# A recurrent attention and two routed mixtures: a chunk's output rows move ahead of the next chunk's values, and the places of the first mixture wait three turns longer

## The chip, the cores and the metric

The kernel runs on one core of one Trainium2 chip. The metric is the device time of one launch in microseconds. Three runs of the kernel before gave 523.09, 523.45 and 524.38 us; the median is 523.45 us.

## The reference

Three parts follow each other. The first is a linear attention with a decaying state, for 4 batches, 8 heads, 768 positions and 48 values per head:

```python
for t in range(S):
    state = alpha[:, :, t, :, None] * state + np.einsum('bhd,bhe->bhde', k[:, :, t], v[:, :, t])
    y[:, :, t] = np.einsum('bhd,bhde->bhe', q[:, :, t], state)
```

Its output, seen as 3072 rows of 384 values, goes through a mixture of 8 experts (384 to 1024 to 384, a relu between). Only rows with a positive skip score are computed; each is sent to the expert with the greatest logit and weighted by that expert's probability. The result is added to the row:

```python
logits = xc @ w_gate
e_idx = np.argmax(logits, axis=1)
h = np.maximum(xc[mask] @ w1[e], 0.0)
y[mask] = gate_w[mask, None] * (h @ w2[e])
out[do_compute] = xc + y
```

A second mixture of the same size, without the skip and without the addition, makes the output.

## The kernel before

**Attention.** The positions are cut into 24 chunks of 128 (0 to 23 here), six per batch. The first chunk of a batch has no state to add, and the last one makes none. For chunk g three helpers issue the work. `emit_a(g)` multiplies keys and queries into two PSUM banks, `ap0` and `ap1` (line 566); VectorE masks the first (`at`, line 574), ScalarE copies the second and GpSimd masks it (line 572). Then TensorE transposes the keys (`kp`, line 581) and ScalarE copies them (`ks`). `emit_y(g)` makes the chunk's outputs (`yp`, lines 605 to 615) and the next state (`sp`, lines 599, 610, 611); ScalarE takes both out (`y`, line 618, and `s`, line 623). `emit_r(g)` turns the outputs into rows of 384 values and 17 logits with four matmuls (`rp`, line 645). ScalarE copies the rows to `xy` (line 646), a DMA stores them, and VectorE sums the logits into `lg` (line 648). `prep(g)` runs two scans over alpha on VectorE (lines 546 and 550), and GpSimd multiplies keys and queries with them (lines 554 and 555).

**Order.** Each engine works its instructions off in the order in which the program issues them. One turn of the attention loop (line 747 on) issues `emit_a(g + 1)`, `prep(g + 3)`, `emit_y(g)`, `emit_r(g - 1)`. In the attention the tiles `ap0`, `ap1`, `sp`, `yp` and `rp` share four PSUM banks that are handed out in turn, so a tile waits for the last reader of an earlier one.

**Routing.** Small instructions on VectorE find each row's expert and its place among the expert's rows. They are generators in a list. `rt(n)` moves waiting ones on by a step or more; `release(w)` counts a tick (a turn) up and moves on those that asked for TensorE's turn (`yield 1`) more than w ticks ago; `finish` runs named ones to their end. In the attention a group of rows is routed after chunks 5, 11, 17, 20 and 23. `index` (line 340) ends each: VectorE makes a table `hot` (line 372), and some ticks later TensorE multiplies it into `idx_ps` (line 377). The argument `nl` is 16 for the groups of the attention and 8 for those of the first mixture (`gate_rows`).

**Mixtures.** Nine stages (j from 0 to 8) each put one block of gathered rows through one expert: `ffn1` (lines 463 to 469, `hh` and `hl` are the two halves of the hidden layer), then `ffn2t` (lines 487 to 489). Each tile of weights comes by a DMA into `raw`, and ScalarE with VectorE or GpSimd splits it into two halves (lines 202 and 207). The rows of stage j are routed for the second mixture during the stages behind it. The second mixture has nine stages as well; its first three blocks of rows are gathered (line 441) by what the last routings found.

Of the kernel before, what the change touches and what calls it, by code (L numbers as in the profile page):

```python
# [59 lines left out]
RT1B = (3, 3, 3, 3, 3, 3, 3, 3, 3, 3, 3, 3)  # L60
REL1B = (4, 4, 4, 6, 6, 6, 6, 6, 6, 6, 6, 4)
RELS = (7, 2, 2)
STEPS = (1, 1, 1)
STEPS2 = (3, 2, 3)
FIN2 = (0, 3)
# [43 lines left out]
def body(tc, qka, vN, rw, wg2, wg17, w1a, w2a, w1b, w2b, cst, zr, out):  # L109
# [3 lines left out]
    with ctx:  # L113
# [6 lines left out]
        def cc(name):  # L120
            o, w = CST[name]
            return cs[:, o:o + w]
# [12 lines left out]
        with ExitStack() as fctx, tc.manual_schedule():  # L135
# [25 lines left out]
            def spot(name, w, *shape, bufs=2):  # L161

                if name not in spots:
                    spots[name] = [used[0], 0]
                    used[0] += w * bufs
                    assert used[0] <= 512
                p = spots[name]
                n = int(np.prod(shape))
                assert n <= w
                o = p[0] + w * (p[1] % bufs)  # L170
                p[1] += 1
                v = own[:, o:o + n]
                if len(shape) == 2:
                    v = v.rearrange("p (a b) -> p a b", a=shape[0])
                elif len(shape) == 3:
                    v = v.rearrange("p (a b c) -> p a b c", a=shape[0], b=shape[1])
                return v
# [38 lines left out]
            def background(n=1):  # L216
                for _ in range(n):
                    if bg:
                        split_w(*bg.pop(0))

            active = []
            turn = [0]

            def step(r):
                tok = next(r[0], None)
                if tok is None:
                    active.remove(r)  # L230
                else:
                    r[1] = turn[0] if tok == 1 else None
                return tok != 2

            def rt(n=1):
# [14 lines left out]
            def start(gen):  # L250
                r = [gen, None]
                active.append(r)
                return r

            def finish(*which):

                while any(r in active for r in which):
                    release()
                    rt()
# [61 lines left out]
            def wait(what, i):  # L321

                while done[what] < i:
                    yield 2
# [14 lines left out]
            def index(i, n, nl, ohm, on, rk, cols, region, first, last):  # L339

                ad = sm.tile([128, n, nl], F32, tag=f"ad{nl}", name="ad")
                V.tensor_tensor(ad, rk, ohm, op=ALU.mult)
                held[0] = False
                yield 0
                r = sm.tile([128, n, 1], F32, tag=f"r{nl}", name="r")
                V.tensor_reduce(r[:, :, 0], ad, axis=AX.X, op=ALU.add)
                yield 0
                ge = sm.tile([128, n, 4], F32, tag=f"ge{nl}", name="ge")
                V.tensor_tensor(ge, r.to_broadcast([128, n, 4]), kept["th"].rearrange("p (o e) -> p o e", o=1).to_broadcast([128, n, 4]), op=ALU.is_ge)
                yield 0  # L350

                tl = spot("tl", 6, n, 1)
                V.tensor_reduce(tl[:, :, 0], ge, axis=AX.X, op=ALU.add)
                yield 0
                ti = spot("ti", 48, n, 2, 4)
                V.tensor_tensor(ti, cc("seq")[:, 0:4].rearrange("p (a o e) -> p a o e", a=1, o=1).to_broadcast([128, n, 2, 4]),
                                tl.rearrange("p a (o e) -> p a o e", o=1).to_broadcast([128, n, 2, 4]), op=ALU.is_equal)
                yield 0
                pm = spot("pm", 6, n, 1)
                V.scalar_tensor_tensor(out=pm, in0=tl, scalar=-128.0, in1=r, op0=ALU.mult, op1=ALU.add)  # L360
                w = 8 * sum(t for _, t in cols)
                mv = sm.tile([128, n, 2, w], F16, tag=f"mv{nl}", name="mv")
                o = 0
                for j0, t in cols:
                    V.tensor_tensor(
                        mv.rearrange("p a h c -> p (a h) c")[:, :, o:o + 8 * t].rearrange("p a (e t) -> p a e t", t=t),
                        on.rearrange("p a h e -> p (a h) e")[:, :, j0:j0 + 8].rearrange("p a (e o) -> p a e o", o=1).to_broadcast([128, 2 * n, 8, t]),
                        ti.rearrange("p a h t -> p (a h) t")[:, :, 0:t].rearrange("p a (o t) -> p a o t", o=1).to_broadcast([128, 2 * n, 8, t]), op=ALU.mult)
                    o += 8 * t
                yield 0  # L370
                hot = sm.tile([128, n, 128], F16, tag=f"hot{nl}", name="hot")
                V.tensor_tensor(hot, cc("iota").rearrange("p (o c) -> p o c", o=1).to_broadcast([128, n, 128]), pm.to_broadcast([128, n, 128]), op=ALU.is_equal)
                yield 1
                yield from wait("indexed", i)
                done["indexed"] += 1
                for k in range(n):
                    T.matmul(idx_ps[:, region, :, NCOL - w:], lhsT=hot[:, k, :], rhs=mv[:, k], start=(first and k == 0), stop=(last and k == n - 1))
                if last:
                    yield 0
                    yield 0  # L380
# [152 lines left out]
            def load_v(g):  # L533
                if g >= NB:
                    return
                vt[g] = wk.tile([128, NP, 2 * D], F32, tag="v", name="v", bufs=4)
                SY.dma_start(vt[g], vN[g])
# [181 lines left out]
            def halves_of(w, hi, lo):  # L719
                A.activation(out=hi, in_=w, func=AF.Copy, scale=SX)  # L720
                V.scalar_tensor_tensor(out=lo, in0=w, scalar=SX, in1=hi, op0=ALU.mult, op1=ALU.subtract)
# [26 lines left out]
            for g in range(NB):  # L748
                if g + 1 < NB:
                    emit_a(g + 1)  # L750
                if g + 3 < NB:
                    prep(g + 3, whole)
                emit_y(g)
                if g > 0:
                    emit_r(g - 1)
                    i, k, n, _ = gof[g - 1]
                    if k == n - 1:
                        finish(*routes[max(i - 2, 0):max(i - 1, 0)])
                        routes.append(start(route(i)))
                if g == 0:  # L760
                    A.activation(out=upper, in_=cc("upper"), func=AF.Copy)
                    A.activation(out=ones, in_=cc("ones"), func=AF.Copy)
                    for name, w in (("desc", 8), ("tok", NB), ("seq", 8)):
                        kept[name] = spot(name, w, w, bufs=1)
                        V.tensor_copy(kept[name], cc(name))
                    nb = NB + len(TILES1)
                    kept["th"] = spot("th", 4, 4, bufs=1)
                    V.tensor_copy(kept["th"], cc("th")[:, 1:5])
                    kept["num"] = spot("num", 2 * nb, nb, 2, bufs=1)
                    V.tensor_scalar(kept["num"][:, :, 0], cc("pcol").to_broadcast([128, nb]), 1.0, None, op0=ALU.add)  # L770
                    V.tensor_copy(kept["num"][:, :, 1], cc("blk"))
                    kept["one"] = spot("one", 1, 1, bufs=1)
                    V.memset(kept["one"], 1.0)
                if g == 3:
                    halves_of(wg2s, rg[:, :, 128:136], rg[:, :, 136:144])
                    for k in range(3):
                        P.tensor_copy(rg[:, k, 0:128], ident)
                load_v(g + 3)
                load_qka(g + 5)
                if g >= NB - 2:  # L780
                    turn1(0, g - NB + 2)
                if g == NB - 1:
                    emit_r(g)
                    finish(*routes[:-1])
                    routes.append(start(route(len(GROUPS) - 1)))
                rt(RT[g])
                if g in (3, 6):
                    load_w(0, g // 6)
                if g >= 6 and g % 2 == 0:
                    background()  # L790
# [125 lines left out]
            def tick(f):  # L916
                release(REL1[f] if j == 0 else RELS[min(j, 2)])
                background(f % 2 if j > 1 else 0)
                rt(RT1[f] if j == 0 else STEPS[min(j, 2)])

# [312 lines left out]
```

## Time and profile before

| | |
|---|---|
| median of three runs | 523.45 us |
| the profiled execution, whole | 524.4 us |
| its span, first to last instruction | 522.7 us |
| TensorE busy (matmuls) | 490.9 us, 94% |
| VectorE busy | 353.7 us, 68% |
| ScalarE busy | 270.3 us, 52% |
| GpSimd busy | 267.2 us, 51% |

Busy times are sums over the whole span. The attention fills the first 149 us, the first mixture reaches to about 287 us, the second fills the rest. The profile's names are PE for TensorE's matmuls, DVE for VectorE, ACT for ScalarE and POOL for GpSimd; L574 is line 574 of the kernel before. An entry in square brackets is how long the engine stood idle ahead of the instruction, and what ended that.

### The profile page before, as it was taken

To read this page: it belongs to the slowest core of one execution; us is meant where nothing else is said; L and a number is where in the kernel's file an instruction comes from. 1 tells how busy PE (TensorE), PEld (TensorE's weight loads), DVE (VectorE), ACT (ScalarE), POOL (GpSimd) and SP (SyncE) were. 2 spreads that over 40 slices of the span, in tenths; PEclk is the share of its full clock that TensorE was granted. 3 is DMA by queue.
4 is the path that set the end of the run, shared out by engine and by line. 5 is a ranking of instruction groups with operands and counts; after the bars stand their busy time and mean duration, and the time that the engine had idled before them with its cause. 6 is when DMAs were issued, how large, how long until landed. Compare 5 with 4: busy or idle time off the path is not lost.

```text
span 522.7 us, 12038 instructions
## 1 busy us (share of the span) xinstructions
PE 490.9 (94%) x4701; PEld 378.2 (72%) x4701; DVE 353.7 (68%) x927; ACT 270.3 (52%) x546; POOL 267.2 (51%) x226
## 2 busy tenths in 40 slices
PE   5899998999988999999989989999999999999995
PEld 2688887888878899998979657565555566666663
DVE  7958997989877776877688845853736363636430
ACT  2355554655634666666556324744546464647431
POOL 3477769689726866697866252326215051402022
PEclk9799999999999999999999999999999999999998
DMA  8689686392355858677873167573544527171011
GB/s 294 253 268 327 225 293 227 118 295 95 80 172 167 291 173 297 218 241 241 256 265 124 50 215 271 173 255 93 169 150 130 196 82 251 55 267 44 1 41 42
DMA packets 44868, 96.74 MB, mean 185 GB/s; under 512 B 7049, under 2 KB 31879, under 8 KB 44806
## 3 DMA queue, kind: packets, MB, share of 16 engines
q1 hardware_dynamic: 36614, 77.68, 45.2%
q0 software_dynamic: 4736, 13.51, 7.7%
q10 hardware_dynamic: 3456, 4.72, 2.5%
q8 instruction: 39, 0.64, 0.5%
q14 instruction: 23, 0.19, 0.1%
HBM read 83.41 MB, written 12.99 MB: 184 GB/s over the span
## 4 chain that ended last, share of the span: by engine, by line
PE 61%; DVE 20%; issue 7%; POOL 5%; DMA 4%; ACT 2%; POOLq 0%; ACTq 0%; DVEq 0%
PE hp L464 8%; PE hp L463 8%; PE hp L465 8%; PE ypc L487 4%; PE ypc L488 4%; PE ypc L489 4%; DVE pp L546 3%; DVE qka L550 3%; PE yp L488 3%; PE yp L489 3%; PE yp L487 3%; PE tp L450 3%; DMA xg<-xrows,ixb 2%; PE ap L566 2%; PE rp L645 2%
## 5 line engine op out<-in xcount | busy, mean ns | idle before, releaser
L983 POOL DMA_INDIRECT out<-o,ixo x31 | 31.4, 1013 | 141.9 <-ACT o L1058 119.6
L469 DVE SCALAR_TENSOR_TENSOR h2l<-hp,h2h 128x352 f16<-128x352 f32 (+8 forms) x66 | 38.6, 585 | 63.7 <-ACT h2h L468 62.7
L465 PE MATMUL hp<-x2h,w0l 128*128 128x352 f16 (+8 forms) x216 | 68.7, 323 | 0.0
L463 PE MATMUL hp<-x2h,w0h 128*128 128x352 f16 (+8 forms) x216 | 68.7, 323 | 0.0
L464 PE MATMUL hp<-x2l,w0h 128*128 128x352 f16 (+8 forms) x216 | 68.7, 323 | 0.0
L468 ACT ACTIVATE h2h<-hp 128x352 f16<-128x352 f32 (+8 forms) x66 | 33.8, 514 | 46.8 <-PE hp L465 46.7
L202 ACT ACTIVATE w0h<-raw 128x768 f16<-128x768 f32 x64 | 53.4, 836 | 4.9 <-DMA raw<-in_w1a 1.9
L207 POOL TENSOR_TENSOR w1l<-raw,w1h 128x768 bf16<-128x768 f32 (+1 forms) x26 | 43.1, 1682 | 22.8 <-ACT w1h L202 18.8
L441 POOL DMA_INDIRECT xg<-xrows,ix x41 | 48.6, 1185 | 11.6 <-issue 9.3
L463 PE MATMUL hp<-xh,w0h 128*128 128x200 f16 (+7 forms) x216 | 52.4, 252 | 2.0 <-DVE hl L469 0.9
L202 ACT ACTIVATE w1h<-raw 128x768 f16<-128x768 f32 x64 | 51.5, 837 | 4.4 <-DMA raw<-in_w2a 2.1
L465 PEld LDWEIGHTS <-w0l 128*128 128x128 bf16 x432 | 42.3, 98 | 15.8 <-issue 0.9
L464 PEld LDWEIGHTS <-w0h 128*128 128x128 f16 x432 | 42.3, 98 | 15.7 <-issue 2.3
L488 PE MATMUL yp<-hl,w1h 128*128 128x200 f16 (+7 forms) x216 | 52.6, 252 | 0.6 <-DVE hl L469 0.5
L464 PE MATMUL hp<-xl,w0h 128*128 128x200 f16 (+7 forms) x216 | 52.3, 252 | 0.7 <-DVE xl L452 0.5
L487 PE MATMUL yp<-hh,w1h 128*128 128x200 f16 (+7 forms) x216 | 52.7, 252 | 0.1
L489 PE MATMUL yp<-hh,w1l 128*128 128x200 f16 (+7 forms) x216 | 52.6, 252 | 0.0
L463 PEld LDWEIGHTS <-w0h 128*128 128x128 f16 x432 | 42.3, 98 | 14.0 <-issue 0.6
L465 PE MATMUL hp<-xh,w0l 128*128 128x200 f16 (+7 forms) x216 | 52.4, 252 | 0.0
L554 POOL TENSOR_TENSOR qka<-qka 128x512 f32<-128x512 f32 (+1 forms) x24 | 28.5, 1188 | 38.7 <-DVE qka L550 35.1
L207 DVE TENSOR_TENSOR w0l<-raw,w0h 128x768 bf16<-128x768 f32 x38 | 38.7, 1018 | 13.5 <-ACT w0h L202 11.3
L207 POOL TENSOR_TENSOR w0l<-raw,w0h 128x768 bf16<-128x768 f32 (+1 forms) x26 | 44.3, 1720 | 5.2 <-ACT w0h L202 3.9
(184 smaller groups left out, 1334.2 us busy)
## 6 DMA issues: line engine op xcount, KB each, us to landing
qka<-in_qka SPq DMA_DIRECT2D x21, 772.0 KB, 7.2
raw<-in_w1a SPq DMA_DIRECT2D x8, 1536.0 KB, 6.9
raw<-in_w2a SPq DMA_DIRECT2D x8, 1536.0 KB, 8.7
raw<-in_w1b SPq DMA_DIRECT2D x8, 1536.0 KB, 7.2
raw<-in_w2b SPq DMA_DIRECT2D x8, 1536.0 KB, 7.0
v<-in_vN SPq DMA_DIRECT2D x24, 192.0 KB, 4.2
xrows<-xy ACTq DMA_DIRECT2D x24, 192.0 KB, 4.2
xrows<-x SPq DMA_DIRECT2D x9, 197.0 KB, 5.5
```

What stands on the lines that cost most here:

```text
L202: A.activation(out=hi[:, sl], in_=r[:, sl], func=AF.Copy)
L207: eng.tensor_tensor(lo[:, sl], r[:, sl], hi[:, sl], op=ALU.subtract)
L441: P.indirect_dma_start(out=dst, out_offset=None, in_=xrows[0:rows], in_offset=bass.IndirectOffsetOnAxis(ap=ix, axis=0), bounds_check=rows ...
L463: T.matmul(hp[:, i], lhsT=wh[:, k, f], rhs=xh[:, k, 0:n], start=(k == 0), stop=False)
L464: T.matmul(hp[:, i], lhsT=wh[:, k, f], rhs=xl[:, k, 0:n], start=False, stop=False)
L465: T.matmul(hp[:, i], lhsT=wl[:, k, f], rhs=xh[:, k, 0:n], start=False, stop=(k == 2))
L468: A.activation(out=hh[:, f0:f0 + nf, 0:n], in_=hp, func=AF.Relu)
L469: V.scalar_tensor_tensor(out=hl[:, f0:f0 + nf, 0:n], in0=hp, scalar=0.0, in1=hh[:, f0:f0 + nf, 0:n], op0=ALU.max, op1=ALU.subtract)
L487: T.matmul(yp, lhsT=wh[:, f, ds], rhs=hs[0][:, f, c0:c1], start=(f == 0), stop=False)
L488: T.matmul(yp, lhsT=wh[:, f, ds], rhs=hs[1][:, f, c0:c1], start=False, stop=False)
L489: T.matmul(yp, lhsT=wl[:, f, ds], rhs=hs[0][:, f, c0:c1], start=False, stop=(f == 7))
L983: ins = P.indirect_dma_start(out=out, out_offset=bass.IndirectOffsetOnAxis(ap=ix, axis=0), in_=src, in_offset=None, bounds_check=N - 1, oo ...
```

## The change

It has two parts. In the loop over the chunks `emit_y(g)` moves behind the block that issues `emit_r(g - 1)` and starts a group's routing. So the rows of chunk g - 1 come right behind the transposes of chunk g + 1, ahead of the outputs of chunk g. And `index` asks with `yield 3` where it is called for the first mixture (`nl == 8`): the tick that is noted is then three higher, and `release` moves it on three ticks later. The added lines shift the line numbers by 2 from line 63 on, and by 3 from line 226 on.

```diff
+LAG = 3
...
                 else:
-                    r[1] = turn[0] if tok == 1 else None
+                    r[1] = turn[0] + (tok == 3) * LAG if tok in (1, 3) else None
                 return tok != 2
...
                 V.tensor_tensor(hot, cc("iota").rearrange("p (o c) -> p o c", o=1).to_broadcast([128, n, 128]), pm.to_broadcast([128, n, 128]), op=ALU.is_equal)
-                yield 1
+                yield 3 if nl == 8 else 1
                 yield from wait("indexed", i)
...
                     prep(g + 3, whole)
-                emit_y(g)
                 if g > 0:
                     emit_r(g - 1)
                     i, k, n, _ = gof[g - 1]
                     if k == n - 1:
                         finish(*routes[max(i - 2, 0):max(i - 1, 0)])
                         routes.append(start(route(i)))
+                emit_y(g)
```

On TensorE, in the turn of chunk 3 (g = 3), before; `ap_425` is the second bank of chunk 4's keys by queries:

```order
L566 MATMUL ap_425<-qka 128x128 [waits Activation_49]
...
L581 MATMUL kp<-cs,qka 128x128 x4
L599 MATMUL sp<-s,cs 128x192 [waits Activation_49]
L605 MATMUL yp<-at,v 64x128 [waits DMAHW1_49,DVE_49]
L606 MATMUL yp<-at,v 48x128 [waits Pool_49]
...
L645 MATMUL rp<-rws,y 128x113 [waits DVE_49]
```

The same place now:

```order
L569 MATMUL ap_425<-qka 128x128 [waits DVE_49]
...
L584 MATMUL kp<-cs,qka 128x128 x4
L648 MATMUL rp<-rws,y 128x113 [waits Activation_49]
L648 MATMUL rp<-rws,y 128x113 x3
L602 MATMUL sp<-s,cs 128x192 [waits Activation_49]
L608 MATMUL yp<-at,v 64x128 [waits DMAHW1_49,DVE_49]
L609 MATMUL yp<-at,v 48x128 [waits Pool_49]
```

The rows `rp` stand between the transposes and `sp`. With the order of the tiles the banks change hands differently. Before, `ap_425` took its bank from a `yp` that ScalarE empties, and now from the `rp` of the turn before, whose last reader is VectorE's `lg` of chunk 1. And `yp` took its bank from an `rp` (VectorE's `lg` of chunk 1), and now takes it from this turn's `ap0`, which VectorE's `at` of chunk 4 empties.

On VectorE, in the turn after a group's routing has begun (g = 7 to g = 8), from one `lg` to the next `at`, before:

```order
L648 TENSOR_REDUCE lg<-rp 128x17
L330 TENSOR_TENSOR cum<-cum,own 128x16
L284 TENSOR_REDUCE own<-ex 128x12
L286 TENSOR_SCALAR own<-own 128x12
L289 RECIPROCAL gw<-own 128x12
L677 TENSOR_TENSOR gw<-gw,own 128x12
L574 TENSOR_TENSOR at<-ap_802,cs 128x512
```

And now:

```order
L651 TENSOR_REDUCE lg<-rp 128x17
L333 TENSOR_TENSOR cum<-cum,own 128x16
L287 TENSOR_REDUCE own<-ex 128x12
L289 TENSOR_SCALAR own<-own 128x12
L292 RECIPROCAL gw<-own 128x12
L338 TENSOR_TENSOR on<-ohm,own 128x192
L345 TENSOR_TENSOR ad<-rk,ohm 128x96
L680 TENSOR_TENSOR gw<-gw,own 128x12
L349 TENSOR_REDUCE r<-ad 128x6
L577 TENSOR_TENSOR at<-ap_816,cs 128x512
```

Three more of the routing's small instructions stand between `lg` and `at`; they stood behind `at` before.

On VectorE, in stage 7 of the first mixture, where the routing of stage 5 ends, before (`hl` is the lower half of stage 7's hidden layer, `w0l` a split of the next expert's weights, `x` the output rows of stage 6):

```order
L469 SCALAR_TENSOR_TENSOR hl<-hp,hh 128x2x208
L207 TENSOR_TENSOR w0l_4104<-raw_0_3918,w0h_4103 128x768
L356 TENSOR_TENSOR own<-cs,own 128x16
L469 SCALAR_TENSOR_TENSOR hl<-hp,hh 128x2x208
L360 SCALAR_TENSOR_TENSOR own<-own,r 128x2
L365 TENSOR_TENSOR mv<-on,own 128x128
L842 TENSOR_REDUCE own<-tpb 128x8 x2
L844 SCALAR_TENSOR_TENSOR l_4158<-own,xg 128x8 x2
L848 SCALAR_TENSOR_TENSOR x_3945<-tpb,own,xg 128x384 x2
L469 SCALAR_TENSOR_TENSOR hl<-hp,hh 128x2x208
L372 TENSOR_TENSOR hot<-cs,own 128x256
L469 SCALAR_TENSOR_TENSOR hl<-hp,hh 128x2x208
```

And now:

```order
L363 SCALAR_TENSOR_TENSOR own<-own,r 128x2
L368 TENSOR_TENSOR mv<-on,own 128x128
L375 TENSOR_TENSOR hot<-cs,own 128x256
L472 SCALAR_TENSOR_TENSOR hl<-hp,hh 128x2x208
L209 TENSOR_TENSOR w0l_4110<-raw_0_3918,w0h_4109 128x768
L472 SCALAR_TENSOR_TENSOR hl<-hp,hh 128x2x208
L845 TENSOR_REDUCE own<-tpb 128x8 x2
L847 SCALAR_TENSOR_TENSOR l_4160<-own,xg 128x8 x2
L851 SCALAR_TENSOR_TENSOR x_3948<-tpb,own,xg 128x384 x2
L472 SCALAR_TENSOR_TENSOR hl<-hp,hh 128x2x208
```

`hot` has moved ahead of all four `hl` and of the split.

## Rows read from the trace of the kernel before

**Rows 1.** Stretches of the attention: length, each engine's busy time (count), clock, DMA.
```profile
48.14:88.27 40.13, 36.11 (x502) 31.32 (x502) 36.02 (x65) 22.03 (x56) 31.40 (x23) 1.00 0.75 247
...
sum 111.37, PE 105.92 PEld 92.02 DVE 97.97 ACT 61.63 POOL 87.26; mean PE 35.31 PEld 30.67 DVE 32.66 ACT 20.54 POOL 29.09
```
**Rows 2.** TensorE's waits by releaser: us in total, times, longest.
```profile
PE idx_ps L377 <- DVE hot L372: 5.9, 5, 2.4
...
PE ap L566 <- POOL qka L555: 1.7, 2, 1.1
...
PE yp L606 <- POOL at L572: 1.6, 1, 1.6
```
**Rows 3.** TensorE in a quiet chunk (g = 2): start, length, instruction.
```profile
27.08 1.16 PE L566 MATMUL ap<-qka 64*128 64x128 f32 x16
...
31.56 1.15 PE L645 MATMUL rp<-rws,y 112*128 112x113 f32 x8
32.63 1.16 PE L566 MATMUL ap<-qka 64*128 64x128 f32 x16
```
**Rows 4.** VectorE in the same chunk.
```profile
28.27 0.69 DVE L574 TENSOR_TENSOR at<-ap,cs 128x512 f32<-128x512 f32 x1
28.88 1.23 DVE L546 TENSOR_TENSOR_SCAN pp<-qka,bz 128x520 f32<-128x520 f32 x1
...
30.36 1.27 DVE L550 TENSOR_TENSOR_SCAN qka<-qka,bz 128x520 f32<-128x520 f32 x1
33.45 0.23 DVE L648 TENSOR_REDUCE lg<-rp 128x17 f32<-128x68 f32 x1 [1.82 <-ACT xy L646]
```
**Rows 5.** All engines in a chunk with GpSimd close behind (g = 6).
```profile
49.74 1.19 POOL L555 TENSOR_TENSOR qka<-qka,pp 128x512 f32<-128x512 f32 x1
...
49.94 2.09 DVE L546 TENSOR_TENSOR_SCAN pp<-qka,bz 128x520 f32<-128x520 f32 x1
```
**Rows 6.** VectorE where a group's routing ends (g = 9 to g = 10).
```profile
69.53 0.68 DVE L574 TENSOR_TENSOR at<-ap,cs 128x512 f32<-128x512 f32 x1
...
72.77 0.20 DVE L648 TENSOR_REDUCE lg<-rp 128x17 f32<-128x68 f32 x1
72.89 0.68 DVE L574 TENSOR_TENSOR at<-ap,cs 128x512 f32<-128x512 f32 x1
```
**Rows 7.** TensorE, keys by queries of chunks 11, 17 and 23.
```profile
70.53 1.16 PE L566 MATMUL ap<-qka 64*128 64x128 f32 x16
...
105.42 1.16 PE L566 MATMUL ap<-qka 64*128 64x128 f32 x16
...
138.45 1.16 PE L566 MATMUL ap<-qka 64*128 64x128 f32 x16
```
**Rows 8.** TensorE, places of the first mixture from stages 3, 5 and 8.
```profile
231.82 0.23 PE L377 MATMUL idx_ps<-mv,hot 128*128 128x64 f16 x2 [0.81 <-DVE hot L372]
...
265.14 0.23 PE L377 MATMUL idx_ps<-mv,hot 128*128 128x64 f16 x2 [2.41 <-DVE hot L372]
...
301.81 0.23 PE L377 MATMUL idx_ps<-mv,hot 128*128 128x64 f16 x2 [1.05 <-DVE hot L372]
```
**Rows 9.** VectorE in stage 7, around the second of these.
```profile
260.22 0.96 DVE L207 TENSOR_TENSOR w0l<-raw,w0h 128x768 bf16<-128x768 f32 x1 [1.80 <-ACT w0h L202]
...
264.17 0.58 DVE L469 SCALAR_TENSOR_TENSOR hl<-hp,hh 128x416 f16<-128x416 f32 x1
264.67 0.41 DVE L372 TENSOR_TENSOR hot<-cs,own 128x256 f16<-128x256 f32 x1
265.00 0.58 DVE L469 SCALAR_TENSOR_TENSOR hl<-hp,hh 128x416 f16<-128x416 f32 x1
```
**Rows 10.** The chain that ended last, behind the third of these.
```profile
303.70 7.20 DMA xg<-xrows,ixb
...
310.95 0.55 PE tp L450 x3
```

## The prediction

> **What bounds the kernel now.** I read the stretches first, then TensorE's waits, then one chunk on each engine, then the places of the mixture. From the third chunk on TensorE has little to give: between 27.08 and 138.45 us it is busy for 105.92 of 111.37 us, idle for 5.45 [rows 1]. But VectorE is nearly as full where groups are routed, 36.02 of 40.13 us in the second stretch, as much as TensorE's 36.11 [rows 1]. So the attention has two bounds at a time, and what matters is which of the two has to wait for the other in each turn. In the mixtures TensorE is the bound, and its largest named wait there is for the routing's table: 5.9 us in five places [rows 2].
>
> **The rows' new place, in a quiet chunk.** TensorE works on the same matmuls in either order, 32.63 - 27.08 = 5.55 us for a whole turn [rows 3]. What changes is who lends banks to whom. The order of the instructions says that chunk g + 1's second bank of keys by queries (`ap1`) now waits for VectorE's `lg` of chunk g - 2, the last thing that VectorE does in the turn before; until now it waited for ScalarE's `y`. And `yp` waits for VectorE's `at` of the same turn. In a quiet turn this fits: from the end of `ap` (27.08 + 1.16 = 28.24) to the next `ap` at 32.63 there are 4.4 us, and VectorE needs 28.27 to 31.63 for mask and scans [rows 4] and 0.23 for `lg`, 3.6 us with them. Until now it stood still for 1.82 us ahead of `lg`, because the rows came last [rows 4]; that idle time goes, but in such a turn nobody waits for it. Cost 0, cover 0.8 us. The scan takes 2.09 us in place of 1.23 where GpSimd's multiplication (from 49.74) runs into it [rows 5]: 0.86 more, and the cover is gone.
>
> **The same in a turn with routing.** Here VectorE is behind. At the end of the first group's routing `at` starts at 69.53 and the `lg` that follows at 72.77 [rows 6], while TensorE has begun the next chunk's `ap` at 70.53 [rows 7], ahead of that `lg`. So VectorE found its next input ready and went straight on at 72.89 [rows 6]. In the new order this `ap` needs the `lg`: it starts at about 73.0, 2.5 us later, and VectorE's next `at` at 73.0 + 1.16 + 0.03 = 74.2, 1.3 us later than 72.89. Each turn in which VectorE is behind now has such a hole, 1.2 us less the small instructions that stand between `lg` and `at`. Behind the first three `lg` of a routing stand 1.0 to 3 us of them, which fill most of it (three more of them stand behind the second now); behind the later ones stand none.
>
> I carried this on turn by turn, with the durations of VectorE's rows in each, both conditions on banks, and a scan and a GpSimd instruction never at once. TensorE's `ap` comes out at 73.0 for chunk 11, at 89.4 for chunk 14 (88.27 before [rows 1]: only 1.1 later, since the 1.6 us and a part of the 1.7 us that TensorE waited there for GpSimd [rows 2] are covered by the delay), at 108.5 for chunk 17 (3.1 later than 105.42 [rows 7]) and at 143.6 for chunk 23 (5.2 later than 138.45 [rows 7]). The waits that make this up are 0.7 to 1.5 us in some ten turns. The same carrying with the old order ends 2.0 us later than the trace does, so the difference of the two is 3.2. I take 4.5 us, nearer to the upper, because most of the chunks in which VectorE is behind have their scans lengthened in the trace. Lower bound: with every scan at its shortest (1.23 and 1.27 [rows 4]) chunk 23 comes out at 137.5, 0.9 us early. Upper bound: with every scan as long as in the trace and no GpSimd wait covered, 145.9, 7.4 us late.
>
> Behind chunk 23 the rows of the last two chunks come in the same order as before, but for chunk 22's, ahead of chunk 23's outputs: 0.3 us may be lost as chunk 23's rows wait for ScalarE's copy of its outputs; this is inside the bounds. Stores and loads on the queues keep their order.
>
> **The places.** Three of the five waits have rows: 0.81, 2.41 and 1.05 us [rows 8]. The two others, 5.9 - 4.27 = 1.6 us, belong to stages 2 and 4. There the order shows `idx_ps` at the same matmul and `hot` behind the same ones: the next stage runs the routing to its end before its second product, which cancels the three ticks. They stay. For stages 3 and 5 the two or three ticks that such a forced end counts up let the next routing begin earlier, and `hot` moves ahead of the stage's `hl`. Stage 3: 0.81 goes. Stage 5: `hot` is ready long before, but VectorE was late for another reason, the split at 260.22 that waited for weights [rows 9]. TensorE would begin the second product at 265.14 - 2.41 = 262.73 and after about 1 us, at 263.8, needs the `hl` that ends at 264.75 [rows 9]; with `hot` (0.41) and the two instructions before it gone from ahead of it, it ends some 0.5 us earlier, at 264.25. So 0.45 of the 2.41 stays, 1.95 goes. The weights of the next stage are not earlier for it, and I count 0.5 us of the gain as given back there. Stage 8: the three ticks move `idx_ps` six matmuls on, 1 us, and TensorE no longer waits at 301.81. But the gather that follows (303.70, 7.20 us) starts from VectorE's `hot`, which is where it was, and TensorE waits for its rows at 310.95 [rows 10]; the 1.05 us is waited there. Together 0.8 + 1.9 - 0.5 = 2.2 us gained. Bounds: 0.8 (stage 5's wait wholly turns into one for `hl`) and 3.2 (both go).
>
> **Sum.** +4.5 - 2.2 = +2.3 us on the profiled execution's 524.4 us, of which 1.7 lie outside the span: 526.7. This execution is 0.95 us above the median of 523.45, so a median of 525.8 us.
>
> **Rivals.** First: VectorE's holes pay for themselves. GpSimd's two multiplications come right behind the scans; with a hole there they are over before the next scan, and scans fall back to 1.23 us. Rows 4 speak for it (a turn with a hole of 1.8 us has both scans short), rows 5 show what is to be had. The Trainium skill, SBUF — State Buffer, section "Who interferes with whom", has it as a rule that VectorE's instructions with two inputs in SBUF and GpSimd's reads exclude each other for a whole instruction; by that the lengthening belongs to the overlap, not to the scan, as the rows here have it. Then the attention is 0.9 us shorter, the places give 2.8, and the median is 523.45 - 3.7 = 519.8; with half of it 521 to 522. It decides as soon as the holes are longer than about 1 us, the time that GpSimd's second multiplication still needs when the next `at` is through. Against it: in stretches with weight splits on GpSimd a third instruction follows. Chance 0.2.
>
> Second: the two effects cancel. About half of the scans come out short, the attention loses only 2 us, between the 0.9 gained and the 5.2 lost above, and the places give 2: 523.5. Rows 4 and 5 bear out either half. Chance 0.25.
>
> Third: the ticks do nothing useful (stage 5's wait passes to `hl`, 0.8 gained) and the attention loses its upper value: 523.45 + 7.4 - 0.8 = 530.1. For it: the split at 260.22 waits for a load, which no order cures. Chance 0.1, and for the forecast itself (between 1.6 and 5 us slower) 0.45.
>
> **How the numbers follow.** A difference of 0.3% (1.6 us) is about what a measurement of this kernel can tell. Slower is the forecast and the third rival, 0.55; within 0.3% the second, 0.25; faster the first, 0.2. The likeliest one's own range is 525.0 to 528.5. The range for 8 in 10 reaches into the first rival and takes in most of the third: 520.8 to 529.8.
>
> **What would show it.** Right: `ap` idle for 0.7 to 1.5 us in some ten turns, released by VectorE's `lg`; VectorE idle about 1 us ahead of `at` in chunks 11 to 14 and 17 to 20; chunk 23's `ap` at 141.5 to 144; `idx_ps` waiting 0.5 and 1.1 us for stages 2 and 4 and not for 3 and 5; a longer wait of `tp` for the gathered rows, about 2.1 us in place of 1.1. Wrong: scans of 1.23 us throughout between 50 and 130 us, TensorE idle for 5 us or less from chunk 3 to chunk 23, or a wait of 2 us in stage 7 under another name.

## The result, and the profile after

The changed kernel took 529.56 us (median of four runs, 528.04 to 530.79), beside 523.27 for the kernel before on the same chip. The ratio is 1.0123, with a 95% interval of 1.0087 to 1.0160: 6.4 us slower (4.6 to 8.4). The forecast was 2.3 us slower, between 1.6 and 5, with a median of 525.0 to 528.5 us as the likeliest and 520.8 to 529.8 as the wide range: the measured one lies above the first and 0.2 us inside the second. The profiled execution is the fastest of the four, 528.04 us with a span of 526.3.

First TensorE's waits of the changed kernel from 20 us on, by releaser (us in total, times, longest), against [rows 2] (`rk` is a matmul of the routing too, ahead of `idx_ps`, and `ohm` its input):

```profile
PE idx_ps L380 <- DVE hot L375: 5.8, 5, 2.7
PE ap L569 <- DVE lg L651: 4.5, 5, 1.9
PE ap L569 <- POOL qka L558: 1.4, 2, 0.9
...
PE rk L315 <- DVE ohm L667: 0.9, 1, 0.9
```

The wait of `ap` for `lg` is new, 4.5 us in five places, and the 1.6 us of `yp` for GpSimd is gone. The total of `idx_ps` reads as before, 5.8 for 5.9, but three of its five places are now in the attention, where none was:

```profile
68.28 0.39 PE L380 MATMUL idx_ps<-mv,hot 128*128 128x96 f16 x5 [0.76 <-DVE hot L375]
...
103.58 0.30 PE L380 MATMUL idx_ps<-mv,hot 128*128 128x96 f16 x3 [0.89 <-DVE hot L375]
...
139.12 0.34 PE L380 MATMUL idx_ps<-mv,hot 128*128 128x96 f16 x4 [0.89 <-DVE hot L375]
```

The end of a routing counts ticks too. With the rows ahead of the outputs, the tick at which these matmuls come up is the one right behind `ap`, and no longer the one behind the outputs: TensorE comes to them one block of outputs earlier.

The keys by queries of chunks 11, 17 and 23 [rows 7]:

```profile
72.80 0.56 PE L569 MATMUL ap<-qka 64*128 64x128 f32 x2
...
108.10 0.47 PE L569 MATMUL ap<-qka 64*128 64x128 f32 x2
...
143.63 0.38 PE L569 MATMUL ap<-qka 64*128 64x128 f32 x2
```

I had carried them to 73.0, 108.5 and 143.6. That agrees within 0.4 us and is partly luck, as the start shows. The clock of the execution before, in the stretch from chunk 2's `ap` to chunk 3's (columns: stretch, length, busy time of each engine with counts, granted clock, DMA share, GB/s):

```profile
17.39:27.08 9.69, 8.82 (x79) 7.62 (x79) 8.59 (x16) 2.15 (x6) 4.91 (x5) 0.65 0.48 187
```

A clock of 0.65 says that TensorE ran at the lower of its two levels (1.2 in place of 2.4 GHz) for most of it. The execution after began chunk 3 at 24.25, 2.8 us earlier. So the two are to be compared from chunk 3's `ap` on. By the end of chunk 23's rows the kernel before has used 148.62 - 27.08 = 121.54 us and the changed one 154.22 - 24.25 = 129.97: 8.4 us more, not 5.2. The changed kernel, from `ap` of chunk 3 to that of 8, 14, 20 and to the end of the rows:

```profile
24.25:53.27 29.02, 26.91 (x353) 23.69 (x351) 20.20 (x29) 13.80 (x37) 19.88 (x19) 0.94 0.75 254
53.27:87.58 34.31, 31.64 (x445) 27.84 (x441) 31.02 (x59) 19.32 (x52) 27.19 (x21) 1.00 0.80 259
87.58:123.01 35.43, 32.92 (x441) 29.02 (x442) 30.58 (x60) 18.21 (x47) 23.93 (x20) 0.95 0.66 206
123.01:154.22 31.21, 28.20 (x380) 24.16 (x381) 24.08 (x81) 16.02 (x45) 18.36 (x16) 1.00 0.23 60
sum 129.97, PE 119.67 PEld 104.70 DVE 105.89 ACT 67.36 POOL 89.37; mean PE 29.92 PEld 26.17 DVE 26.47 ACT 16.84 POOL 22.34
```

TensorE is busy longer too (119.67 us, 116.09 before), though it has the same matmuls. Two things add to its busy time. A block of `ap` whose second bank comes late is cut in two, which together are busy 0.48 + 1.16 us in place of 1.16, so such a wait costs more than its entry in brackets: from first start to last end the 21 blocks of chunks 3 to 23 take 8.8 us more than 1.16 each, 0.04 in the kernel before. Seven of them are 0.48 to 2.43 us longer, five others 0.04 to 0.18. And in two places the clock fell. Both happened in chunk 3, on TensorE, with `rp` (L648) at 1.89 us for the usual 1.04 to 1.15:

```profile
24.25 0.48 PE L569 MATMUL ap<-qka 64*128 64x128 f32 x2
26.68 1.16 PE L569 MATMUL ap<-qka 64*128 64x128 f32 x14 [1.95 <-DVE lg L651]
27.76 0.90 PE L584 MATMUL kp<-cs,qka 128*128 128x128 f32 x4
28.46 1.89 PE L648 MATMUL rp<-rws,y 112*128 112x113 f32 x8
```

and the two stretches at half clock (same columns as above):

```profile
28.04:31.45 3.41, 3.41 (x20) 2.97 (x20) 3.34 (x5) 1.57 (x3) 2.39 (x2) 0.50 0.02 9
...
89.48:92.89 3.41, 3.41 (x21) 3.19 (x18) 2.57 (x6) 2.10 (x4) 3.18 (x3) 0.50 0.49 197
```

Ahead of the first TensorE had waited 1.95 us, ahead of the second 0.85 us before a block of `ap` and 0.74 us inside it. The Trainium skill, TensorE: Matmul & The Clock Gate, section "A second HAM failure mode: psum-queue depth-cycling", tells of a kernel with bf16 matmuls that go round the PSUM banks, in which frequent short idle times between groups of them made the clock fall and rise again. The rows here agree in that short waits came ahead of each fall, but these are single waits, among f32 matmuls, with one fall behind them.

Behind the attention the changed kernel is faster: 526.33 - 154.22 = 372.1 us, for 374.1 before. Its places of stages 2 to 5 [rows 8]:

```profile
220.69 0.23 PE L380 MATMUL idx_ps<-mv,hot 128*128 128x64 f16 x2 [0.56 <-DVE hot L375]
...
235.32 0.22 PE L380 MATMUL idx_ps<-mv,hot 128*128 128x64 f16 x2
...
254.08 0.23 PE L380 MATMUL idx_ps<-mv,hot 128*128 128x64 f16 x2 [2.75 <-DVE hot L375]
...
267.77 0.22 PE L380 MATMUL idx_ps<-mv,hot 128*128 128x64 f16 x2
```

Stages 3 and 5 no longer wait, and stage 4 waits 2.75 us in place of 1.1. The reason stands on VectorE, ahead of stage 4's `hot`: a split that waits for ScalarE's, and that one for its load, as [rows 9] showed it in stage 7, now stands here.

```profile
248.20 0.84 ACT L204 ACTIVATE w0h<-raw 128x768 f16<-128x768 f32 x1 [1.96 <-DMA raw<-in_w1a]
249.08 1.01 DVE L209 TENSOR_TENSOR w0l<-raw,w0h 128x768 bf16<-128x768 f32 x1 [2.20 <-ACT w0h L204]
...
252.04 1.14 DVE L851 SCALAR_TENSOR_TENSOR x<-tpb,own,xg 128x384 f32<-128x384 f32 x2
253.10 0.60 DVE L472 SCALAR_TENSOR_TENSOR hl<-hp,hh 128x432 f16<-128x432 f32 x1
253.62 0.41 DVE L375 TENSOR_TENSOR hot<-cs,own 128x256 f16<-128x256 f32 x1
```

Stage 8's `idx_ps` waits 0.08 us, and the gathered rows [rows 10] are waited for less, not more (the first line is of the kernel before):

```profile
310.95 0.44 PE L450 MATMUL tp<-cs,xg 128*128 128x128 f32 x2 [1.11 <-DMA xg<-xrows,ixb]
```
```profile
308.35 1.04 POOL L444 DMA_INDIRECT xg<-xrows,ixb  x1 [12.47 <-DVE own L912]
```
```profile
314.21 0.44 PE L453 MATMUL tp<-cs,xg 128*128 128x128 f32 x2 [0.69 <-DMA xg<-xrows,ixb]
```

They come 5.9 us behind the issue, where it was 7.2.

### The profile page after: what moved, and what is told of

Its sections match the earlier page's. It is cut to its first block, busy times and chain, and to the rows that moved or that the text cites. A ratio compares the mean times of both kernels' runs of the same rounds, so it can differ in the third digit from the quotient of the medians.

```text
span 526.3 us, 12045 instructions
## 1 busy us (share of the span) xinstructions
PE 491.4 (93%) x4701; PEld 380.0 (72%) x4701; DVE 353.6 (67%) x927; ACT 269.1 (51%) x546; POOL 264.4 (50%) x226
## 4 chain that ended last, share of the span: by engine, by line
PE 60%; DVE 24%; issue 5%; DMA 5%; POOL 3%; ACT 2%; POOLq 0%; SPq 0%; DVEq 0%; ACTq 0%
PE hp L467 7%; PE hp L468 7%; PE hp L466 7%; DVE qka L553 5%; DVE pp L549 4%; PE ypc L490 4%; PE ypc L491 4%; PE ypc L492 4%; PE yp L491 2%; PE tp L453 2%; PE yp L492 2%; PE yp L490 2%; PE rp L648 2%; PE ap L569 2%; PE yp L617 2%
```

## Experiments

Of each profiled execution I took the attention from chunk 3's `ap` to the end of chunk 23's rows (before 121.54, changed 129.97), TensorE's busy time in it, the stretches at half clock in it (before none), and what was left behind it (before 374.1, changed 372.1). Times in us; a ratio is to the kernel before on the same chip.

| run | ratio (95%) | attention | TensorE busy | half clock | behind it |
|---|---|---|---|---|---|
| changed kernel | 1.0123 (1.0087 to 1.0160) | 129.97 | 119.67 | 2 | 372.1 |
| e_rows | 1.0176 (1.0148 to 1.0203) | 129.96 | 119.70 | 2 | 375.3 |
| e_lag | 0.9967 (0.9941 to 0.9993) | 120.95 | 116.40 | 0 | 376.3 |
| e_bank | 1.0098 (1.0060 to 1.0137) | 126.82 | 113.72 | 0 | 377.5 |
| e_bank_lag | 1.0007 (0.9979 to 1.0034) | 123.11 | 116.60 | 0 | 373.8 |
| e_tick | 1.0291 (1.0259 to 1.0323) | 129.76 | 119.48 | 1 | 384.4 |
| e_bank_tick | 1.0204 (1.0169 to 1.0238) | 124.11 | 113.91 | 0 | 382.4 |
| e_copy | 1.0138 (1.0109 to 1.0167) | 127.34 | 114.85 | 1 | 373.9 |
| e_copy_tick | 1.0116 (1.0082 to 1.0149) | 125.51 | 116.83 | 2 | 374.1 |
| e_lag4 | 0.9947 (0.9928 to 0.9965) | 120.91 | 116.38 | 0 | 377.2 |
| e_lag5 | 0.9928 (0.9895 to 0.9962) | 120.93 | 116.39 | 0 | 369.8 |
| e_after5 | 1.0051 (1.0019 to 1.0082) | 129.91 | 118.63 | 1 | 369.4 |
| e_hold5 | 1.0071 (1.0044 to 1.0097) | 127.68 | 117.80 | 1 | 370.2 |

**The two parts apart.** e_rows has the rows' place alone, e_lag the ticks alone (edits are shown against the changed kernel).

```diff
-LAG = 3
+LAG = 0
```


> The rows' new place alone, the ticks as before. Theory 1 (the bank: chunk g + 1's ap waits for VectorE's lg of chunk g - 2): the attention ends 5 to 6 us later than before (rows of chunk 23 end at about 154 in place of 148.6) with waits of ap for lg of some 4.5 us in five places, and the two parts add up: about 2 us above the changed kernel, 530 to 532. Theory 2 (the 2 us that the mixtures won back in the changed kernel are no work of the ticks, but slack: weights and gathers are further along when a stage begins later): the time is that of the changed kernel, 528 to 530, without the ticks.

```diff
+                emit_y(g)
                 if g > 0:
                     emit_r(g - 1)
...
-                emit_y(g)
```


> The ticks alone, the rows where they were before. Theory 1 (the places are worth 2.2 us by themselves: stage 3's wait of 0.81 goes, stage 5's falls from 2.41 to about 0.45, stages 2 and 4 keep 0.54 and 1.09): 521.1, attention unchanged with its last rows at 148.6. Theory 2 (slack): the mixture wins nothing, the waits reappear at weights and gathers: 523.3, within 0.5 of before.

In time and attention theory 1 held in both, though what e_lag won, 0.4 to 3.1 us, doesn't quite leave out theory 2 (within 0.5 of before). The rows' place alone costs 1.76%, 9.2 us; its attention has the waits, the stretches at half clock and the length of the changed kernel. The ticks alone win 0.33% (1.7 us, 0.4 to 3.1). In e_rows the places wait 0.54, 0.82, 1.75, 1.35 and 1.05 us, in e_lag 0.54, none, 2.60, none and 0.08: theory 1 had 1.09 for stage 4. The 376.3 of e_lag's profiled execution holds two stretches at half clock, of 3.4 us each, at 163 and 249 us.

**The bank.** e_bank is the changed kernel, e_bank_lag the old order with the ticks, both with this:

```diff
-                    kp = bank("K", "kp", NP, GP)
+                    kp = bank("B", "kp", NP, GP)
...
-                rp = bank("B", "rp", NP, 113)
+                rp = bank("K", "rp", NP, 113)
```


> The changed kernel, with the rows in the bank that kp had, and kp in the ring of four; so ap's second bank comes from kp (freed by ScalarE a turn earlier) and the rows' bank from lg a whole turn earlier. Theory 1 (the bank): the waits of ap for lg (4.5 us in 5) go, chunk 23's ap falls from 143.6 to 138 to 140, and with the places' gain the time is 522 to 525. Theory 2 (VectorE and GpSimd are the bound, whichever instruction meets them): the same microseconds come back as waits of yp for VectorE's at and of ap for GpSimd's qka, chunk 23's ap stays at 142 to 144, time 528 to 530. Theory 3 (the clock): whatever the waits, stretches at half clock follow wherever TensorE stands still for over 1 us; without such waits none shows after 30 us.

> The old order with the ticks, and the same exchange of banks as in the run before: ap no longer waits for anything of the turn before. Theory 1 (banks bind only in the new order): as with the ticks alone, 521 to 522. Theory 2 (VectorE and GpSimd are the bound): the same 521 to 522, with waits of ap for GpSimd's qka of 1.7 us as before; under 520 would say that the old order too lost time to its banks.

No theory came out whole. `ap` waits for no `lg` any more, as theory 1 had it, its blocks are no longer cut (0.04 us in all), and no stretch at half clock is left, but the attention falls by 3.2 us only. In their place TensorE waits for the routing:

```profile
PE idx_ps L380 <- DVE hot L375: 4.6, 3, 1.7
PE rk L315 <- DVE ohm L667: 2.8, 2, 2.2
```

Theory 3 fails in one half: TensorE stands still for 1.54, 1.73, 2.15 and 1.37 us here, and no half clock follows.

The old order lost 2.2 us of attention to the exchange (123.11 for 120.95), so the exchange itself is not free: its trace has waits of `yp` for the two `at` that e_lag's hasn't, 2.7 us (VectorE) and 1.5 us (ScalarE) in three places each.

**The routing's place.** e_tick gives the changed kernel one turn more for the routing's matmuls in the attention, e_bank_tick has that and the exchange. (4 is a tick more; `hold` has the same.)

```diff
-                yield 3 if nl == 8 else 1
+                yield 3 if nl == 8 else 4
```


> The changed kernel, with the routing's matmuls of the attention (rk and idx_ps) one of TensorE's turns later than they stand there. Theory 4 (two things add up: ap waits for lg through the bank, and the rows' new place brings the routing's matmuls ahead of their inputs; idx_ps waits for hot 2.5 us in three and rk for ohm 0.95 in one): the second part goes, the rows of chunk 23 end at about 151 in place of 154.2, time 526 to 527 by the better runs; the lg waits of 4.5 us stay, and with them the two stretches at half clock near 28 and 89 us. Theory 2 (VectorE and GpSimd are the bound, whatever TensorE meets): the waits come back as ap for lg or for qka, the rows still end at 153 to 154, time 528 to 530.

> The exchange of banks and the routing's matmuls one turn later, both. In the run with the exchange alone the lg waits were gone, but idx_ps waited for hot 4.6 us in three and rk for ohm 2.8 in two, and the rows of chunk 23 ended at 151.0, 5.7 later than in the old order with the ticks. Theory 4 (bank and routing's place together are the loss): these waits go too, the rows end at 145.5 to 147.5, time 521.5 to 524. Theory 2 (VectorE and GpSimd are the bound in the new order): the rows stay at 150 to 151, time 526 to 529.

As whole kernels both are worse, for a reason that I had not foreseen: the last group got the turn too, and the gather behind it came 10.4 us late for TensorE.

```profile
180.21 0.63 PE L453 MATMUL tp<-cs,xg 80*128 80x80 f32 x3 [10.45 <-DMA xg<-xrows,ixb]
```

In the attention e_tick did what theory 2 said: no wait for `hot`, but 8.2 us for `lg` in 11 places, and nearly the same length. With the exchange, the tick brings 2.7 us: the rows end at 148.2, between what theory 4 and theory 2 had. So neither cure helps much while the other cause stands (3.2 and 0.2 us), and both bring 5.9. By stretches of the same chunks as in the changed kernel, e_bank and then e_bank_tick:

```profile
24.16:50.47 26.31, 24.80 (x353) 21.75 (x351) 23.11 (x29) 14.19 (x41) 22.46 (x19) 1.00 0.85 282
...
84.50:119.79 35.29, 30.86 (x442) 27.12 (x442) 30.31 (x60) 18.12 (x48) 23.84 (x20) 1.00 0.67 207
119.79:150.98 31.19, 27.24 (x380) 23.58 (x381) 24.11 (x81) 16.16 (x45) 18.35 (x16) 1.00 0.22 60
```
```profile
24.08:50.22 26.14, 24.79 (x353) 21.75 (x351) 22.95 (x29) 14.15 (x41) 22.29 (x19) 1.00 0.87 292
...
85.81:118.29 32.48, 30.66 (x441) 27.02 (x441) 29.33 (x53) 17.14 (x45) 26.97 (x20) 1.00 0.69 218
118.29:148.19 29.90, 27.24 (x380) 23.57 (x381) 23.75 (x77) 16.02 (x45) 18.43 (x16) 1.00 0.24 63
```

The first stretch (29.02 in the changed kernel) is cured by the bank alone, the third (35.43) only by the routing's place with it, the last (31.21) in part.

**The bank in another way.** ScalarE copies the logits out, so that the bank is not VectorE's to free; e_copy_tick adds the tick, without the last group.

```diff
-                V.tensor_reduce(lg[:, g, :], rp[:, :, 96:113].rearrange("p a b -> p b a"), axis=AX.X, op=ALU.add)
+                lc = wk.tile([128, NP, 17], F32, tag="lc", name="lc")
+                A.activation(out=lc, in_=rp[:, :, 96:113], func=AF.Copy)
+                V.tensor_reduce(lg[:, g, :], lc.rearrange("p a b -> p b a"), axis=AX.X, op=ALU.add)
```


> The changed kernel, with the logits copied out of the rows' bank by ScalarE (68 columns, an estimate of 0.25 us each from its 48-column copies of 0.31) and reduced by VectorE from the copy, so that ap's bank is freed by ScalarE behind xy and no longer by VectorE's lg; banks and order otherwise as they are. From chunk 3's ap to the end of chunk 23's rows the changed kernel takes 130.0 us, 3.4 of it in two stretches at half clock (1.7 us lost in each), the old order 121.0. Theory 4 (bank and routing's place together; the half clock follows the waits of 1 to 2 us for lg): no lg wait and no stretch at half clock near 28 and 89 us, but idx_ps and rk wait for VectorE as with the exchange of banks, 4 to 7 us; the stretch takes 124 to 126.5, time 525 to 528. Theory 2 (VectorE and GpSimd bound): 128 to 130, time as the changed kernel's. If the stretches at half clock stay where they were without the waits, they have another cause.

> The same, and the routing's matmuls of the attention one of TensorE's turns later, but not for the last group (where the turn cost 10.4 us at the gather behind the attention in the two runs before). Theory 4: nothing is left to wait for; from chunk 3's ap to the end of chunk 23's rows 121 to 123.5 us as in the old order, and the time is that of the old order with three ticks, 521.5 to 524. Theory 2: 126 to 129 us, time 526 to 529.

In the attention e_copy fell between its theories: no wait of `ap` for `lg`, 2.6 us less, 3.7 us for `hot` and 2.7 for `ohm` instead, no half clock near 28 and 89 but one stretch at 129 us, behind a wait of 2.08 us for `ohm`. As a whole it is no faster than the changed kernel. e_copy_tick missed theory 4's 121 to 123.5 by 2.0: its waits for the routing are gone from the attention, but it has two stretches at half clock, near 87 and 121 us, 4.1 us of `ap` for GpSimd and 3.0 of `yp` for VectorE's `at`, and its time is theory 2's. So what remains after both cures is not settled.

**More ticks.** The old order with four and five (e_lag4 has 4 here).

```diff
-LAG = 3
+LAG = 5
```


> The old order with four ticks in place of three; the routing's matmuls of each stage of the mixture stand six matmuls later once more. With three ticks stage 4 is the one that still waits, 2.6 us, and it would wait some 1.0 less. If what a place wins is kept to the end: 521.0, 1 us under three ticks. If it is given back at the next load of weights or of rows: the same as with three, 522.

> The old order with five ticks. Four gave a ratio to before of 0.9947, three 0.9967, with intervals that overlap. Stage 4 still waited 2.35 us with four. If each tick takes about 0.3 to 1.0 us from that wait and the rest follows: 520.5 to 522, ratio 0.993 to 0.995. If five ticks bring the next routing's rank behind its turn (its matmuls move too), the next hot is late: 523 to 525.

Four ticks left stage 4 a wait of 2.35 us, so the 1.0 of the first forecast did not come, and their ratio can't be told from that of three. Five remove it, and the ratio is 0.9928: 3.8 us faster than before (2.0 to 5.5), a little more than forecast. This version beats both kernels; the intervals of four and five overlap. Stage 4 and 5:

```profile
241.73 0.22 PE L380 MATMUL idx_ps<-mv,hot 128*128 128x64 f16 x2
...
257.17 0.22 PE L380 MATMUL idx_ps<-mv,hot 128*128 128x64 f16 x2
```

Its attention, by the same chunks as in the changed kernel:

```profile
24.35:50.44 26.09, 25.47 (x351) 21.99 (x350) 23.38 (x29) 13.93 (x40) 22.25 (x19) 1.00 0.90 304
50.44:84.94 34.50, 32.00 (x442) 27.64 (x442) 31.04 (x60) 18.64 (x48) 31.67 (x21) 1.00 0.72 242
84.94:117.57 32.63, 31.46 (x442) 27.34 (x442) 30.42 (x59) 18.73 (x48) 25.50 (x20) 1.00 0.73 222
117.57:145.28 27.71, 27.46 (x380) 23.68 (x381) 22.92 (x79) 15.62 (x42) 19.34 (x16) 1.00 0.22 61
```

**Five ticks with the rows' new place, and the clock by itself.** e_after5 is the changed kernel with five ticks. e_hold5 is e_lag5 with two waits put in:

```diff
                 kk, qq = kt[g], qt[g]
+                for _ in range({7: 2, 17: 3}.get(g, 0)):
+                    A.activation(out=qq, in_=qq, func=AF.Copy)
```


> The changed kernel with five ticks in place of three. If the two parts are independent (the rows' place costs what it costs in the attention, the ticks win in the mixtures what they win in the old order): five ticks against three were 517.9 against about 520.4 to 521 in the old order on one chip, so 2.5 to 3.5 us under the changed kernel, 525 to 527, all waits of idx_ps for hot in the mixture gone and the attention as long as with three (130 us from chunk 3's ap to the end of chunk 23's rows, two stretches at half clock). If the gain depends on when a stage begins: 528 to 530.

> The old order with five ticks, and two waits put in by hand: ScalarE copies the queries of chunk 7 twice and of chunk 17 three times in place, so that TensorE has to wait for ap by some 1.8 us near 46 us and some 2.3 us near 102 us (ScalarE is free 0.8 us after ap would begin, its copies take 0.5 each). Nothing else is changed. Theory 3 (TensorE's clock falls where it has stood still): one or both waits are followed by a stretch of 3.4 us at half clock, none of which the old order had between 25 and 148 us in five profiled executions; the time is 518 + 4 for the waits + 1.7 for each such stretch, 522 to 526. Rival (the stretches of the new order belong to something else): no such stretch, 520 to 522, a part of the 4 us being taken up behind it.

e_after5 came out as its first case: what the rows' place costs and what the ticks win add up. It lies 6.4 us above e_lag5 by their ratios and 8.4 by the profiled executions, all of that in the attention (129.91 and 120.93); what is behind it is the same (369.4 and 369.8). It has one stretch at half clock fewer than the changed kernel and the same attention: `ap` waits 0.7 us for `lg` at 95.96, where the changed kernel has no such wait. e_hold5 waited 2.41 us up to 48.09 and 3.33 us up to 107.87. Behind the first, then ahead of the second and behind it:

```profile
48.09:51.50 3.41, 3.41 (x54) 3.07 (x55) 2.18 (x4) 1.77 (x4) 2.81 (x3) 1.00 1.02 379
104.00:107.92 3.92, 0.59 (x7) 0.44 (x6) 2.10 (x4) 2.96 (x8) 2.74 (x3) 1.00 1.03 396
107.92:111.33 3.41, 3.41 (x24) 2.75 (x26) 1.42 (x2) 0.60 (x1) 1.14 (x2) 0.50 0.23 87
```

The longer wait is followed by half clock at once, the shorter one in this execution by none. Nine of the twelve runs had a mean clock of 0.980 to 0.986 and took 525.6 to 529.7 us; the three at 0.992 and 0.993, the profiled one among them, took 523.2 to 524.0. So one wait put in by hand was followed by half clock where the old order has none, and theory 3 stands for that one. The median of 526.92 is above both theories' times. The middle of the nine (527.3) lies 3.5 us above the middle of the three: what a wait costs beside its length is not the same in each run.

## Why the prediction came out as it did

**Sign and mechanism: right.** `ap` waits for `lg` through the bank; e_bank, e_copy and their waits show it. VectorE stood idle ahead of `at` by 1.06, 1.20 and 1.15 us in chunks 11, 12 and 17, but not in the other chunks named. The profile names five waits, not ten; by the length of the blocks seven are much longer and five a little.

**The attention: the term that was too small, 4.5 forecast, 8.4 measured** (9.0 against the old order at full clock, e_lag5), which is more than its upper bound of 7.4. The step that failed is the first, "Cost 0, cover 0.8 us" for a quiet turn. It cost 29.02 - 26.09 = 2.9 us by chunk 8: in chunk 3 VectorE came to `lg` only at 26.43 and TensorE had asked at 24.25; half clock followed. The same `lg`, changed and before:

```profile
26.43 0.20 DVE L651 TENSOR_REDUCE lg<-rp 128x17 f32<-128x68 f32 x1
```
```profile
27.90 0.23 DVE L648 TENSOR_REDUCE lg<-rp 128x17 f32<-128x68 f32 x1 [1.57 <-ACT xy L646]
```

VectorE was ready for it at 26.43 and at 26.33 (27.90 - 1.57), so VectorE came no later than before; it was TensorE that had come later. I had read the cover from [rows 4], where VectorE is idle 1.82 us ahead of `lg` and both scans are short. But that execution had lost 2.8 us of TensorE's time just ahead, so VectorE and GpSimd had had time to get ahead of it. In e_lag5 the scans of the same chunk take 1.73 and 1.82 us and no cover is there; the prediction had seen in [rows 5] that a longer scan takes it away, but counted a quiet turn without one:

```profile
27.05 1.73 DVE L549 TENSOR_TENSOR_SCAN pp<-qka,bz 128x520 f32<-128x520 f32 x1
...
29.02 1.82 DVE L553 TENSOR_TENSOR_SCAN qka<-qka,bz 128x520 f32<-128x520 f32 x1
```

From chunk 8 on the carried numbers held: with 2.9 taken off, chunks 14, 17 and 23 come out 0.2 early, 3.2 and 5.7 late against e_lag5, for 1.1, 3.1 and 5.2 forecast. The absolute times of chunks 11 to 23 agreed only because the execution before had lost 2.8 us just ahead of chunk 3, and the change loses 2.9 just behind it.

**What the term did not have.** The 9.0 us against e_lag5 are 5.8 more of idle time (10.30 for 4.54) and 3.3 more of busy time. In the idle time stand 4.5 us for `lg`, which the term had, and 2.5 for `hot` and 0.9 for `ohm`, which it had not; 3.1 us of waits for GpSimd and for `lg` that e_lag5 has are gone. The waits for `hot` come from the routing's matmuls, which moved as well: I followed the ticks in the mixture, and not that a place ahead of the outputs changes what a tick means in the attention (from e_bank to e_bank_tick that is 2.8 us of the third stretch). In the busy time stand 4.1 us of `ap` whose blocks were cut (28.50 for 24.40) and, by an estimate, some 3 us of half clock beside them (half of 2 x 3.41, less what lies in `ap`); against that, the new order by itself takes 2.9 us less of TensorE's time (113.72 in e_bank for 116.60 in e_bank_lag). So it is luck in part that the carried numbers held from chunk 8 on: the carrying had none of these four, and they go both ways. Between the runs the time goes with the clock: the two above 530 us had 0.983 and 0.988, the two below 529 had 0.990 and 0.992.

**The places: 2.2 forecast, 2.0 measured behind the attention** (2.8 from e_rows and the changed kernel's ratios, 1.7 from e_lag). The size is right, the parts are not. Stage 3 gave its 0.8, as forecast. Stage 5 gave all its wait, since no `hl` took its place. Stage 4, which I had as unchanged at 1.1, rose to 2.75. And stage 8's 1.0 was not waited again at the gather, because the rows came 1.4 us sooner behind their issue. That e_rows has 1.75 and 1.35 in stages 4 and 5 without any tick shows that such waits change without any tick too; that it goes with when a stage begins is argued, not shown.

**The rivals.** None came about whole. The first: the scans did not fall back. The 28 of them between 50 and 130 us take 1.59 us on average in the changed kernel, 1.58 before and 1.54 in e_lag5. The second: the attention lost far more than 2 us. The third named 530.1, nearer to 529.56 than the forecast: the attention lost even more than its 7.4, while the ticks won more than its 0.8. The wide range was said to take in most of it, but ends 0.3 us below; that it holds the measured time is luck more than judgement. The rule of the Trainium skill cited with the first rival (SBUF — State Buffer, "Who interferes with whom") was neither borne out nor contradicted by a run here.

**What stays open.** What is left above the old order in e_copy_tick (4.6 us) and in e_bank_tick (1.0 us with the same banks): their traces name waits of `ap` for GpSimd (4.1 and 3.0 us) and of `yp` for VectorE's `at` (3.0 and 2.4 us), but no run takes these away. And why half clock followed the wait of 1.95 us in the changed kernel, and not the one of 2.41 us in e_hold5's profiled execution or of 2.15 us in e_bank's.

## What to carry to other kernels

Before a cover is read from a trace, look at the granted clock ahead of it: an engine that seems to have slack may only have been waiting for a TensorE at half speed. When instructions that take turns in a ring of banks are reordered, list for each tile which engine frees its bank afterwards, and follow everything else that is placed by counting the same turns. A wait inside a block of matmuls is measured from the block's first start to its last end, since the entry in brackets shows a part of it (4.5 of some 8 us here). Two causes in one turn can hide each other: undoing either alone won 0.2 to 3.2 us of attention here, both 5.9.

## What the runs showed of the hardware

- In the attention behind chunk 3 TensorE's clock fell to its lower level only behind waits of 1.6 to 3.3 us (once two that together make 1.6), for 3.41 us each time, but not behind all: 2.41 us in e_hold5, 2.15 in e_bank and 2.02 in e_copy were followed by none. Between 25 us and the end of the attention the new order had nine in eight profiled executions, the old order none in five, and one more behind the wait put in by hand.
- In a quiet turn the new order is shorter: 5.37 us (39.02 - 33.65) against 5.55 [rows 3]. In e_bank, without half clock, TensorE is busy 113.72 us in the attention for 116.60 in e_bank_lag, with the same matmuls. So the new order by itself is 2.9 us less of TensorE's time, which the waits ate up.
